# A gated mix of linear attention and a long convolution: two chunks of tokens share the transpose of q's last 64 features

## The chip, the cores and the metric

The kernel runs on one core of a Trainium2 chip. A core has five engines, each with its own in-order queue: TensorE (PE in the profile; its weight loads are listed apart as PEld), VectorE (DVE), ScalarE (ACT), GpSimd (POOL) and SyncE (SP, which here only starts DMAs). They meet through semaphores. The metric is the device time of one execution in microseconds (us). Matrix products and transposes write to PSUM, an accumulator memory of 8 banks with 2 KB in each of 128 partitions; everything else lives in SBUF.

## The reference

The input is 2048 tokens of 448 features. Branch A is linear attention with 16 heads of 28 features; branch B is a state-space convolution along the tokens; a gate per token mixes them.

```python
def _A_ref(x, wqkv, wo):
    qkv = (x @ wqkv).reshape(B, S, 3, H, Dh)      # H = 16, Dh = 28
    phi = lambda t: jnp.where(t > 0, t + 1, jnp.exp(t)) + 1e-6
    pq, pk = phi(q), phi(k)
    kv = jnp.einsum("bhsd,bhse->bhde", pk, v)
    z = jnp.einsum("bhsd->bhd", pk)
    num = jnp.einsum("bhqd,bhde->bhqe", pq, kv)
    den = jnp.einsum("bhqd,bhd->bhq", pq, z)[..., None] + 1e-6
    return (num / den).reshape(B, S, D) @ wo
...
g = sigmoid((x * gate_w).sum(-1, keepdims=True))
return g * A(x) + (1 - g) * B(x)
```

What matters here is the last part of A: phi(q), scaled by gate and denominator, times a matrix M of 448 x 448 that has been made of kv and wo.

## The kernel before, in words

The tokens are cut into 16 chunks of 128. A first part (up to about 118 us) projects q and k, and sums the products of k's features with x. A second part (118 to 127 us) makes kv and from it M. The third part, from line 814, is a loop over the 16 chunks that computes the output rows; the change lies in it and in the few lines that start it up.

Products are made at a precision above that of one pass: a number is split into a high part, rounded to the format fp32r by a copy, and a low part, the difference. A product is then high times high, low times high and high times low.

For each chunk c of the third part:

- `norm_a`, `norm_b`, `norm_d` make the reciprocal denominators: POOL multiplies q's features with the sum over k (L542), DVE sums over each head (L547), inverts two chunks at a time (L551, L553), and ACT copies the result to SBUF for POOL (L556).
- `norm_c` writes the scaled features into the tile `pn`, 128 tokens x 4 blocks of 128 columns. Blocks 0 to 2 are written by POOL (L567: 112 columns each) and DVE (L570: the last 16 columns of each). Block 3 holds the 64 features that are left, 16 of each of the last four heads, **twice** (L573, on POOL): columns 0 to 63 and again 64 to 127.
- `turn_pe` transposes the four blocks on PE into one PSUM bank of the pool `tr` (two buffers), so that features lie on partitions (L604).
- `turn_split` splits the bank: ACT copies all 512 columns to the high part `h` (L611), then DVE writes the low part `l` (L612).
- `tail` puts the gate's rows into partitions 64 to 111 of block 3 of `l` (ACT, L615).
- `attend` runs 11 matmuls of 448 columns (L629): high, low and high again of blocks 2, 0 and 1 against `mh`, `mh` and `ml`; then `h` of block 3, and `l` of block 3. In block 3 one pass over 128 partitions does two products at once: the first 64 rows of `h` meet the high part of M, the second copy of them meets M's low part, which lies in partitions 64 to 127 of `mh[:, 3]`. The first matmul needs `h`, the second needs `l`, the tenth and eleventh need block 3.
- `final_b` adds the product to y, with the gate (DVE, L634), and SP writes the rows out; `final_c` copies the product to `pq` (ACT, L640).

The order on each engine is written out by hand: the loop's body issues, for c, `norm_d` for chunks c+3 and c+4 (odd c), `final_b` of c-1, `norm_c` of c+2, `turn` of c+1, `final_c` of c-1, `tail` of c+1, `norm_a` of c+6, `attend` of c and `norm_b` of c+5. So PE transposes chunk c+1 ahead of the matmuls of chunk c, and ACT and DVE have the time of those 11 matmuls to split it. Beside this, `late` finishes the q features of the last chunk between the iterations (DVE's L799 in iteration 6, ACT's L796 in iteration 5).

"Turn c" below is the splitting of chunk c (it is issued in iteration c-1), "attend c" are the matmuls of chunk c.

Of the kernel before, what the change touches and what calls it, by code (L numbers as in the profile page):

```python
# [7 lines left out]
F32 = mybir.dt.float32  # L8
# [3 lines left out]
ALU = mybir.AluOpType  # L12
# [3 lines left out]
P = 128  # L16
S = 2048
D = 448
H = 16
DH = 28  # L20
N = 256
NC = S // P
J = 4
DJ = D // J
# [14 lines left out]
DS = 12  # L39
DT = 4 * (DH - DS)  # L40
# [100 lines left out]
def gated_mix_kernel(ctx: ExitStack, tc: tile.TileContext, xin, wq_d, wvo_d, abc_d, ldt_d, dsk_d,  # L141
                     turn_d, cst_d, first_d, gin_d, out):
    nc = tc.nc
    PE, ACT, DVE, POOL, SP = nc.tensor, nc.scalar, nc.vector, nc.gpsimd, nc.sync

    keep = ctx.enter_context(tc.tile_pool(name="keep", bufs=1))
    pq = keep.tile([P, NC, D], F32, name="pq")
# [59 lines left out]
    o = 0  # L207
    for part in PARTS:
# [8 lines left out]
        o = e  # L217
# [17 lines left out]
    def low(eng, o, r, h):  # L235
        eng.tensor_tensor(out=o, in0=r, in1=h.bitcast(F32), op=ALU.subtract)  # L236
# [301 lines left out]
    pn, th, tl, pd, dn, dp = {}, {}, {}, {}, {}, []  # L538

    def norm_a(c):  # L540
        pd[c] = tp.tile([P, D], F32, name="prod", tag="pk", bufs=3)
        POOL.tensor_tensor(out=pd[c], in0=pq[:, c], in1=zb, op=ALU.mult)  # L542
# [6 lines left out]
    def norm_d(c, n, copy=DVE.tensor_copy):  # L549
        r = dp[0][:, c:c + n]  # L550
        DVE.scalar_tensor_tensor(out=r, in0=r, scalar=1e-6, in1=e1[:, c:c + n, None].to_broadcast([P, n, H]),  # L551
                                 op0=ALU.add, op1=ALU.mult)
        DVE.reciprocal(out=r, in_=r)  # L553
        if c % 2 == 0:
            dn[c // 2] = tp.tile([P, 4, H], F32, name="den", tag="den", bufs=3)
        copy(dn[c // 2][:, c % 2:c % 2 + n], r)  # L556

    def norm_bd(c):
        norm_b(c)
        norm_d(c, 1)  # L560

    def norm_c(c):
        n = pn[c] = tp.tile([P, J, P], F32, name="pn", tag="pn")
        r = dn[c // 2][:, c % 2]
        a = pq[:, c, :3 * DJ].rearrange("p (j h d) -> p j h d", j=3, h=4)
        b = pq[:, c, 3 * DJ:].rearrange("p (h d) -> p h d", h=4)
        POOL.tensor_tensor(out=n[:, :3, :DJ].rearrange("p j (h d) -> p j h d", h=4), in0=a,  # L567
                           in1=r[:, :H - 4].rearrange("p (j h) -> p j h", j=3)[:, :, :, None].to_broadcast([P, 3, 4, DH]),
                           op=ALU.mult)
        DVE.tensor_tensor(out=n[:, :3, DJ:].rearrange("p j (h d) -> p h j d", h=4),  # L570
                          in0=b[:, :, :DS].rearrange("p h (j d) -> p h j d", j=3),
                          in1=dp[0][:, c, H - 4:, None, None].to_broadcast([P, 4, 3, DS // 3]), op=ALU.mult)
        POOL.tensor_tensor(out=n[:, 3].rearrange("p (b h d) -> p b h d", b=2, h=4),  # L573
                          in0=b[:, None, :, DS:].to_broadcast([P, 2, 4, DH - DS]),
                          in1=r[:, None, H - 4:, None].to_broadcast([P, 2, 4, DH - DS]), op=ALU.mult)

    def phi(c):
        if 0 < c < NC:
# [18 lines left out]
    def turn(c):  # L597
        turn_split(c, turn_pe(c))

    def turn_pe(c):  # L600
        o = p3.tile([P, 512], F32, name="tr", tag="tr")
        n = pn.pop(c)
        for j in range(J):
            PE.transpose(o[:, j * P:(j + 1) * P], n[:, j], ident)  # L604
        return o

    def turn_split(c, o):
        t = xt_p.tile([P, 2, J, P], F32R, name="th", tag="t")
        h, l = th[c], tl[c] = t[:, 0], t[:, 1]
        ov = o.rearrange("p (j t) -> p j t", j=J)  # L610
        ACT.copy(h, ov)  # L611
        DVE.tensor_tensor(out=l, in0=ov, in1=h.bitcast(F32), op=ALU.subtract)  # L612

    def tail(c):
        ACT.copy(tl[c][DT:RX, 3], rows[DT:RX, c * P:(c + 1) * P])  # L615
# [26 lines left out]
    c = NC - 2  # L642
# [26 lines left out]
    POOL.memset(rows[DT:RX, :D], 0.0)  # L669
    norm_bd(0)  # L670
    norm_c(0)
    norm_a(2)
    for i in range(4):
# [57 lines left out]
    def kv_split(r, kvp):  # L731
        o = kvp[:DJ, (1 - r) * 2 * DJ:(2 - r) * 2 * DJ].rearrange("p (j d) -> p j d", d=DJ)
        m = 2 - r
        DVE.tensor_tensor(out=o[:, :m], in0=kvp[:DJ, 2 * r * DJ:(2 * r + m) * DJ].rearrange("p (j d) -> p j d", d=DJ),
                          in1=mask[:, None, :].to_broadcast([DJ, m, DJ]), op=ALU.mult)
        if r:
            a, b = (w.rearrange("p (h d) -> p h d", h=4) for w in (kvp[:DJ, 3 * DJ:4 * DJ], mask))
            DVE.tensor_tensor(out=o[:, 1, :DT].rearrange("p (h d) -> p h d", h=4), in0=a[:, :, DS:], in1=b[:, :, DS:],
                              op=ALU.mult)
            a, b = (w[:, :, :DS].rearrange("p h (j d) -> p h j d", j=3) for w in (a, b))  # L740
            DVE.tensor_tensor(out=o[:, 1, DT:].rearrange("p (j h d) -> p h j d", j=3, h=4), in0=a, in1=b, op=ALU.mult)
        return o

    def kv_high(r, o):
        ACT.copy(kvh[:, 2 * r:2 * r + 2], o)
# [6 lines left out]
    k0 = kv_products(0)  # L752
    k1 = kv_split(1, k1)
    kv_high(1, k1)
    norm_c(1)
    norm_a(3)
    kv_low(1, k1)
# [11 lines left out]
    SP.dma_start(out=mh[DT:, 3].bitcast(F32), in_=shl[:DT, 1].bitcast(F32))  # L769
    m_low(2, o2)  # L770
    o0 = turn_pe(0)
    q_run(2)
    norm_a(4)
    turn_split(0, o0)
    norm_b(2)
    norm_b(3)
# [8 lines left out]
    m_low(0, o0)  # L785
    m_low(1, o1)
    norm_c(2)
    tail(0)
    q_run(11)
# [147 lines left out]
```

## Time and profile before

| | |
|---|---|
| time, median of 3 runs | 173.89 us (173.82 to 174.45) |
| the profiled execution, own time | 174.06 us |
| its span, first to last instruction | 172.2 us |
| start of attend 0, end of the last matmul | 126.87 us, 169.10 us |
| transposes (L604) | 64, 272 ns each |
| ACT's copies of 512 columns (L611) | 16, 588 ns each |
| DVE's subtractions of 512 columns (L612) | 16, 691 ns each |
| POOL's writes of block 3 (L573) | 16, 410 ns median |

The profile shows one execution. A line of its timeline gives the start and length in us, the engine, the line of the kernel, the operation, and the tiles that it writes and reads; "x10" is a run of ten, and "[0.32 <-ACT th L611]" is the time that the engine sat idle before it, and what ended that. Since matmuls are pipelined, the listed length of one is longer than the distance from one to the next. The granted TensorE clock is at full speed throughout.

### The profile page before, as it was taken

The numbers are of one execution on the slowest core, as the hardware profiler recorded it, in microseconds if no ns is written. First come the engines' busy times: TensorE is split into PE (matmuls) and PEld (weight loads), VectorE is DVE, ScalarE is ACT, GpSimd is POOL, SyncE is SP. The second block draws the span as 40 slices with busy tenths as digits, with TensorE's granted clock in tenths as the row PEclk, the third lists the DMA queues.
The fourth block names the chain that finished last, engine by engine and source line by source line (L and its number), as shares of the span: only waits on it lengthen the run. The fifth ranks groups of instructions, "written<-read, shape, count | busy, mean of one in ns | idle before, by whom it ended". The sixth has DMA issues, their size and how long they took to land. (4 is left out here: it accounts for less than half of the span.)

```text
span 172.2 us, 2796 instructions
## 1 busy us (share of the span) xinstructions
PE 167.8 (97%) x876; PEld 152.0 (88%) x876; DVE 113.9 (66%) x240; ACT 96.0 (56%) x221; POOL 120.0 (70%) x128
## 2 busy tenths in 40 slices
PE   6999999999999999999999999999999999999992
PEld 2788999999899999999999999999899999999992
DVE  0847737698975483846627346487898998987542
ACT  3688588894256262542727456356574564664541
POOL 6082667877529988696996999529968998892200
PEclk9999999999999999999999999999999999999999
DMA  5989975097003031230404200000031222122213
GB/s 173 415 297 294 268 209 166 0 368 303 4 0 114 11 123 34 95 123 1 122 15 131 106 1 1 0 0 2 7 67 54 107 89 76 62 99 107 108 59 108
DMA packets 7962, 18.60 MB, mean 108 GB/s; under 512 B 2045, under 2 KB 4810, under 8 KB 7818
## 3 DMA queue, kind: packets, MB, share of 16 engines
q1 hardware_dynamic: 7802, 18.30, 32.0%
q8 instruction: 7, 0.11, 0.3%
q10 hardware_dynamic: 144, 0.11, 0.2%
q14 instruction: 9, 0.07, 0.1%
HBM read 14.38 MB, written 3.67 MB: 105 GB/s over the span
## 5 line engine op out<-in xcount | busy, mean ns | idle before, releaser
L629 PE MATMUL a<-wk,th 128*128 128x448 f32 (+1 forms) x170 | 36.4, 360 | 0.0
L403 PE MATMUL g<-pkh,xn 128*128 128x448 f32 x112 | 35.6, 364 | 0.0
L629 PEld LDWEIGHTS a<-wk,th 128*128 128x128 f32 x170 | 29.5, 189 | 1.6
L334 PE MATMUL k<-wk,xt 128*128 128x448 f32 x132 | 29.3, 367 | 0.0
L334 PE MATMUL q<-wqh,xt 128*128 128x450 f32 x120 | 27.5, 366 | 0.0
L362 DVE SCALAR_TENSOR_TENSOR k<-k,e 128x448 f32<-128x448 f32 x12 | 7.6, 632 | 29.4 <-ACT e L361 29.4
L423 POOL TENSOR_TENSOR y<-y,t 128x448 f32<-128x448 f32 x16 | 18.7, 1168 | 11.5 <-DVE t L415 11.5
L334 PEld LDWEIGHTS k<-wk,xt 128*128 128x128 f32 x132 | 24.8, 189 | 2.2 <-DVE wk L236 0.3
L334 PEld LDWEIGHTS q<-wqh,xt 128*128 128x128 f32 x120 | 22.5, 188 | 1.7
L236 POOL TENSOR_TENSOR xn<-xr,xn 128x448 fp32r<-128x448 f32 x16 | 19.4, 1211 | 6.6 <-ACT xn L246 4.5
L403 PE MATMUL g<-pkl,xn 128*128 128x448 f32 x64 | 23.4, 366 | 0.0
L403 PEld LDWEIGHTS g<-pkh,xn 128*128 128x128 f32 x112 | 21.0, 188 | 2.2
L236 POOL TENSOR_TENSOR xt<-xr,xt 128x512 fp32r<-128x512 f32 x14 | 18.2, 1297 | 5.9 <-ACT xt L240 5.9
L360 ACT ACTIVATE e<-k 128x448 f32<-128x448 f32 x12 | 6.5, 544 | 26.9 <-PE k L334 26.9
L542 POOL TENSOR_TENSOR prod<-pq,zb 128x448 f32<-128x448 f32 x16 | 18.6, 1172 | 4.1 <-ACT zb L665 3.0
L252 POOL TENSOR_TENSOR y<-xr,rows 128x448 f32<-128x448 f32 x16 | 18.8, 1175 | 0.0
L567 POOL TENSOR_TENSOR pn<-pq,den 128x336 f32<-128x336 f32 x16 | 12.3, 771 | 5.9 <-ACT den L556 4.1
L634 DVE SCALAR_TENSOR_TENSOR ot<-y,og,a 128x448 f32<-128x448 f32 (+1 forms) x17 | 10.7, 629 | 5.1 <-PE a L629 5.1
L612 DVE TENSOR_TENSOR th<-tr,th 128x512 fp32r<-128x512 f32 x16 | 11.0, 691 | 2.7 <-ACT th L611 2.1
L403 PEld LDWEIGHTS g<-pkl,xn 128*128 128x128 f32 x64 | 11.2, 174 | 1.2 <-DVE pkl L372 0.2
L611 ACT CAST th<-tr 128x512 fp32r<-128x512 f32 x16 | 9.4, 588 | 4.6 <-PE tr L604 4.4
L334 PE MATMUL q<-wql,xt 128*128 128x450 f32 x45 | 11.6, 364 | 0.0
(150 smaller groups left out, 302.3 us busy)
## 6 DMA issues: line engine op xcount, KB each, us to landing
xr<-in SPq DMA_DIRECT2D x15, 512.0 KB, 6.2
out<-ot SPq DMA_DIRECT2D x15, 224.0 KB, 1.9
pq<-in SPq DMA_DIRECT2D x4, 448.0 KB
wvo<-in SPq DMA_DIRECT2D x1, 1792.0 KB
y<-in SPq DMA_DIRECT2D x2, 480.0 KB
y<-in SPq DMA_DIRECT2D x2, 450.0 KB
u<-t SPq DMA_DIRECT2D x30, 1.8 KB, 1.7
y<-in SPq DMA_DIRECT2D x1, 448.0 KB, 4.3
```

Of the source, the lines that this page charges most:

```text
L236: eng.tensor_tensor(out=o, in0=r, in1=h.bitcast(F32), op=ALU.subtract)
L252: POOL.tensor_tensor(out=y[:, c], in0=plain[c][:, :D], in1=dsk, op=ALU.mult)
L334: PE.matmul(o[:, :n], lhsT=a, rhs=b, start=run.n == 1, stop=not seq)
L362: DVE.scalar_tensor_tensor(out=pks[c], in0=pks[c], scalar=1.0, in1=e, op0=ALU.add, op1=ALU.max)
L403: PE.matmul(g[i][:a.shape[1], :D], lhsT=a, rhs=b, start=c == 0 and n == 0, stop=c == NC - 1 and n == len(seq) - 1)
L423: POOL.tensor_tensor(out=y[:, c], in0=y[:, c], in1=t, op=ALU.add)
L542: POOL.tensor_tensor(out=pd[c], in0=pq[:, c], in1=zb, op=ALU.mult)
L567: POOL.tensor_tensor(out=n[:, :3, :DJ].rearrange("p j (h d) -> p j h d", h=4), in0=a, in1=r[:, :H - 4].rearrange("p (j h) -> p j h", j=3)[ ...
L611: ACT.copy(h, ov)
L612: DVE.tensor_tensor(out=l, in0=ov, in1=h.bitcast(F32), op=ALU.subtract)
L629: PE.matmul(a[:, lo:hi], lhsT=u_, rhs=w_[:, lo:hi], start=n == 0, stop=n == 10)
L634: DVE.scalar_tensor_tensor(out=ot[:, lo:hi], in0=y[:, c, lo:hi], scalar=og[:, c:c + 1], in1=a[:, lo:hi], op0=ALU.mult, op1=ALU.add)
```

## The change

Block 3 is written for two chunks at once. For an even chunk c, the new `norm_pair(c)` lets POOL write 64 features of chunk c into columns 0 to 63 and the 64 features of chunk c+1 into columns 64 to 127. After the transpose, partitions 0 to 63 of the bank hold chunk c's rows, and partitions 64 to 127 hold chunk c+1's. An odd chunk transposes three blocks only.

The second copy of the 64 rows in `h` is now made by the engines that split. In an even turn ACT copies all 512 columns, then copies rows 0 to 63 of block 3 once more into partitions 64 to 127 of `h` (over the other chunk's rows). In an odd turn ACT copies the 64 rows from the bank of the chunk before, twice, into both halves of `h`'s block 3; DVE subtracts these 64 rows; then ACT and DVE do the 384 columns of the three other blocks. A list, `halves`, keeps the address of the bank's rows from the even turn to the odd one. For chunk 0 `norm_pair` is called from the start-up part, when the denominators of chunk 1 are there.

```diff
+    def norm_pair(c):
+        b = pq[:, c:c + 2, 3 * DJ:].rearrange("p b (h d) -> p b h d", h=4)
+        POOL.tensor_tensor(out=pn[c][:, 3].rearrange("p (b h d) -> p b h d", b=2, h=4), in0=b[:, :, :, DS:],
+                           in1=dn[c // 2][:, :2, H - 4:, None].to_broadcast([P, 2, 4, DH - DS]), op=ALU.mult)
+
     def norm_c(c):
...
-        POOL.tensor_tensor(out=n[:, 3].rearrange("p (b h d) -> p b h d", b=2, h=4),
-                          in0=b[:, None, :, DS:].to_broadcast([P, 2, 4, DH - DS]),
-                          in1=r[:, None, H - 4:, None].to_broadcast([P, 2, 4, DH - DS]), op=ALU.mult)
+        if c and c % 2 == 0:
+            norm_pair(c)
...
     def turn_pe(c):
         o = p3.tile([P, 512], F32, name="tr", tag="tr")
         n = pn.pop(c)
-        for j in range(J):
+        for j in range(J - c % 2):
             PE.transpose(o[:, j * P:(j + 1) * P], n[:, j], ident)
         return o
 
+    halves = []
+
     def turn_split(c, o):
+        low = lambda l, a, h: DVE.tensor_tensor(out=l, in0=a, in1=h.bitcast(F32), op=ALU.subtract)
+        ov = o.rearrange("p (j t) -> p j t", j=J)
         t = xt_p.tile([P, 2, J, P], F32R, name="th", tag="t")
         h, l = th[c], tl[c] = t[:, 0], t[:, 1]
-        ov = o.rearrange("p (j t) -> p j t", j=J)
-        ACT.copy(h, ov)
-        DVE.tensor_tensor(out=l, in0=ov, in1=h.bitcast(F32), op=ALU.subtract)
+        if c % 2:
+            b = halves.pop()
+            for p in (slice(DT, P), slice(DT)):
+                ACT.copy(h[p, 3], b)
+            low(l[:DT, 3], b, h[DT:, 3])
+            ACT.copy(h[:, :3], ov[:, :3])
+            low(l[:, :3], ov[:, :3], h[:, :3])
+        else:
+            halves.append(ov[DT:, 3])
+            ACT.copy(h, ov)
+            ACT.copy(h[DT:, 3], ov[:DT, 3])
+            low(l, ov, h)
...
     kv_high(1, k1)
+    norm_pair(0)
     norm_c(1)
```

On ACT, turns 3 and 4 stood so before, from the `tail` of chunk 2 on (`rows` is the source of `tail`, `tr` a transposed bank, `th` the tile of `h` and `l`, `a` a product, `den` the reciprocals; the numbers tell buffers apart, th_1462 being chunk 2's, th_1500 chunk 3's):

```order
L615 CAST th_1462<-rows_77 48x128
L556 COPY den_1473<-den_1276 128x32
L611 CAST th_1500<-tr_1495 128x512
L640 COPY pq_58<-a_1475 128x448
L615 CAST th_1500<-rows_77 48x128
L556 COPY den_1523<-den_1276 128x32
L611 CAST th_1537<-tr_1532 128x512
L640 COPY pq_58<-a_1508 128x448
```

The same stretch of ACT now; L627 is the old L611, L657 the old L640, L632 the old L615, and th_1501 is chunk 3's tile:

```order
L632 CAST th_1463<-rows_77 48x128
L556 COPY den_1475<-den_1276 128x32
L621 CAST th_1501<-tr_1458 64x128 x2
L623 CAST th_1501<-tr_1497 128x384
L657 COPY pq_58<-a_1477 128x448
L632 CAST th_1501<-rows_77 48x128
L556 COPY den_1527<-den_1276 128x32
L627 CAST th_1540<-tr_1535 128x512
L628 CAST th_1540<-tr_1535 64x128
L657 COPY pq_58<-a_1512 128x448
```

The odd turn 3 has three copies in place of one, the first two out of chunk 2's bank (tr_1458), and the even turn 4 has a second copy behind the first. Nothing else on ACT has changed its place.

On DVE, turns 3 and 4 before (the row of `tr` is the subtraction):

```order
L634 SCALAR_TENSOR_TENSOR ot_1488<-y_59,og_62,a_1475 128x448
L570 TENSOR_TENSOR pn_1491<-pq_58,den_1276 128x4x3x4
L612 TENSOR_TENSOR th_1500<-tr_1495,th_1500 128x512
L547 TENSOR_REDUCE den_1276<-prod_1467 128x16
L551 SCALAR_TENSOR_TENSOR den_1276<-den_1276,e1_61 128x32
L553 RECIPROCAL den_1276<-den_1276 128x32
L634 SCALAR_TENSOR_TENSOR ot_1525<-y_59,og_62,a_1508 128x448
L570 TENSOR_TENSOR pn_1528<-pq_58,den_1276 128x4x3x4
L612 TENSOR_TENSOR th_1537<-tr_1532,th_1537 128x512
```

And now:

```order
L651 SCALAR_TENSOR_TENSOR ot_1490<-y_59,og_62,a_1477 128x448
L575 TENSOR_TENSOR pn_1493<-pq_58,den_1276 128x4x3x4
L614 TENSOR_TENSOR th_1501<-tr_1458,th_1501 64x128
L614 TENSOR_TENSOR th_1501<-tr_1497,th_1501 128x384
L547 TENSOR_REDUCE den_1276<-prod_1469 128x16
L551 SCALAR_TENSOR_TENSOR den_1276<-den_1276,e1_61 128x32
L553 RECIPROCAL den_1276<-den_1276 128x32
L651 SCALAR_TENSOR_TENSOR ot_1529<-y_59,og_62,a_1512 128x448
L575 TENSOR_TENSOR pn_1532<-pq_58,den_1276 128x4x3x4
L614 TENSOR_TENSOR th_1540<-tr_1535,th_1540 128x512
```

The odd turn has two subtractions in place of one, at the same place. On POOL the write of block 3 is gone from odd chunks and follows L572 (the old L567) for even ones; for chunk 0 it has moved behind the next L542.

## The prediction, made before the changed kernel was run

> **What bounds the kernel now.** I read the page's busy times first:
>
> ```profile
> PE 167.8 (97%) x876; PEld 152.0 (88%) x876; DVE 113.9 (66%) x240; ACT 96.0 (56%) x221; POOL 120.0 (70%) x128
> ```
>
> PE is busy for 97% of the span, and DVE's 66% is a mean over stages. So I read a table by stretches, with cuts near the starts of attends 0, 6 and 10 (columns: stretch, length, then busy us of each engine):
>
> ```profile
> 126.50:142.60 16.10, 16.10 (x93) 14.91 (x92) 14.60 (x34) 9.13 (x25) 14.84 (x22) 1.00 0.24 84
> 142.60:153.20 10.60, 10.60 (x62) 9.75 (x61) 9.88 (x25) 5.54 (x15) 9.48 (x13) 1.00 0.19 72
> 153.20:172.20 19.00, 15.90 (x99) 14.80 (x97) 10.18 (x22) 8.34 (x21) 3.62 (x7) 1.00 0.26 95
> ```
>
> PE never stops in the loop, but until 153 us DVE is nearly full too: 14.60 of 16.10 us, then 9.88 of 10.60. Only the last stretch leaves it air. The waits from 118 us on say who waits for whom:
>
> ```profile
> DVE ot L634 <- PE a L629: 5.1, 7, 0.9
> ACT th L611 <- PE tr L604: 4.4, 6, 1.0
> DVE th L612 <- ACT th L611: 2.1, 7, 0.4
> PEld m L708 <- DVE kvl L748: 0.2, 1, 0.2
> ```
>
> DVE and ACT wait for PE; PE waits for nobody in the loop (its one wait, 0.2 us, is before it). So the end is set by PE's own work, as long as DVE delivers `l` in time. The prediction is a race between a shorter PE and a later DVE.
>
> **What PE gains.** From one attend to the next:
>
> ```profile
> 131.61 0.37 PE L629 MATMUL a<-rc,th 112*128 112x448 f32 x1
> 131.82 0.60 PE L604 MATMUL tr<-both,pn 128*128 128x128 f32 x4
> 132.18 2.26 PE L629 MATMUL a<-wk,th 128*128 128x448 f32 x10
> ...
> 131.62 0.57 PEld L604 LDWEIGHTS tr<-both,pn 128*128 128x128 f32 x4
> 132.15 0.30 PEld L629 LDWEIGHTS a<-wk,th 128*128 128x128 f32 x2
> ...
> 153.10 0.27 PE L589 MATMUL o<-both,og 128*1 128x128 f32 x1
> 153.22 0.60 PE L604 MATMUL tr<-both,pn 128*128 128x128 f32 x4
> ```
>
> Four transposes occupy 132.18 - 131.82 = 0.36 us, 0.09 each, although each is listed with 0.27. The loads go at (132.15 - 131.62)/4 = 0.13, and a lone extra matmul of 128 columns takes 153.22 - 153.10 = 0.12. So one transpose is worth 0.09 to 0.13 us; I take 0.09, from the matmuls themselves. Eight odd chunks lose one each: **8 x 0.09 = 0.72 us** (up to 1.06).
>
> **What the small instructions cost.** DVE and ACT rows of other sizes give the price by length:
>
> ```profile
> L612 DVE TENSOR_TENSOR th<-tr,th 128x512 fp32r<-128x512 f32 x16 | 11.0, 691 | 2.7 <-ACT th L611 2.1
> 121.65 0.39 DVE L748 TENSOR_TENSOR kvl<-k,kvh 112x224 fp32r<-112x224 f32 x1 [0.36 <-ACT kvh L745]
> 122.09 0.17 PEld L708 LDWEIGHTS m<-wo,kvl 112*112 112x112 f32 x1 [0.15 <-DVE kvl L748]
> L611 ACT CAST th<-tr 128x512 fp32r<-128x512 f32 x16 | 9.4, 588 | 4.6 <-PE tr L604 4.4
> L640 ACT COPY pq<-a 128x224 f32<-128x224 f32 x2 | 0.6, 348 | 2.0 <-DVEq L847 2.0
> 120.39 0.27 DVE L734 TENSOR_TENSOR k<-k,cst 112x112 f32<-112x112 f32 x1
> 120.70 0.23 DVE L738 TENSOR_TENSOR k<-k,cst 112x64 f32<-112x64 f32 x1
> ```
>
> DVE: (0.691 - 0.392)/288 = 1.04 ns per column, so 384 columns take 0.56 and 128 take 0.29. ACT: (0.588 - 0.348)/288 = 0.83 ns, so 384 take 0.48 and 128 take 0.27. No row shows ACT or DVE writing other partitions than it reads: I bound the 64x128 copy by nothing and by the whole 0.59, and take 0.27, the nearest by size. PE's load started 122.09 - 122.04 = 0.05 after the subtraction it waited for. An instruction that needs its predecessor on its own engine starts about 0.04 after that one's end (120.70 against 120.66); the even turn's second copy overwrites rows of the first, so it is one: **an even turn's `h` is ready 0.04 + 0.27 = 0.31 us later**, and every DVE instruction behind L612 with it.
>
> An odd turn's two small copies need nothing new and could go early, but ACT's queue is `tail`, then they, then the 384 columns. Independent ACT copies follow each other at some 0.07 us less than their length (estimate), so the two take 0.4, and the copy ends 0.4 + 0.48 - 0.59 = 0.29 later where ACT is late, and DVE's 384 columns end 0.29 - 0.13 = 0.16 later. Where DVE is itself the late one, its two subtractions cost 0.29 + 0.56 - 0.08 overlap (estimate) - 0.69 = **0.08**.
>
> The Trainium skill, Perfetto Trace Analysis, "Optimizing Scalar/DVE Operations", speaks against such splitting: each DVE instruction on PSUM carries about 125 ns of access overhead, so larger ones are to be preferred. By that price the odd turn would cost 0.125 and not 0.08, and the lag at turn 4 would be 0.05 larger; no run so far shows the split itself.
>
> **The race, turn by turn.** The rows of turns 1 and 4:
>
> ```profile
> 127.29 0.30 ACT L615 CAST th<-rows 48x128 fp32r<-48x128 f32 x1
> 127.61 0.59 ACT L611 CAST th<-tr 128x512 fp32r<-128x512 f32 x1
> 128.23 0.69 DVE L612 TENSOR_TENSOR th<-tr,th 128x512 fp32r<-128x512 f32 x1
> ...
> 135.82 0.59 ACT L611 CAST th<-tr 128x512 fp32r<-128x512 f32 x1
> 136.44 0.69 DVE L612 TENSOR_TENSOR th<-tr,th 128x512 fp32r<-128x512 f32 x1
> ...
> 137.47 0.30 PEld L629 LDWEIGHTS a<-wk,th 128*128 128x128 f32 x2
> ```
>
> In turn 1 ACT goes straight from `tail` to the copy, so it is the late one: lag 0.16. In turn 2 ACT waits for PE, which is 0.09 earlier: lag 0.31 - 0.09 = 0.22. Turn 3 adds 0.08: 0.30. In turn 4 L612 started 0.03 after ACT's copy: + 0.31, so **lag 0.61**. Attend 4 loads `l` as its second weight, at 137.47 + 0.30 - 0.19 = 137.58; `l` was ready at 137.13 + 0.05: slack 0.40. PE therefore ends turn 4 at 0.61 - 0.40 = 0.21 *after* its old time, having spent the 0.27 of turns 1, 3 and 5. Part of this is paid one step earlier: the transposes of chunk 4 overwrite the bank of chunk 2, which DVE's small subtraction of turn 3 still reads; the 11 matmuls of attend 3 queue behind them.
>
> From turn 5 to 7 DVE catches up (it waits for PE there), and PE gains 2 x 0.09 by turn 9. Now turns 8 and 10:
>
> ```profile
> 144.54 1.23 POOL L542 TENSOR_TENSOR prod<-pq,zb 128x448 f32<-128x448 f32 x1
> 144.97 1.05 DVE L799 TENSOR_SCALAR t<-e 128x448 f32<-128x448 f32 x1
> 147.33 0.69 DVE L612 TENSOR_TENSOR th<-tr,th 128x512 fp32r<-128x512 f32 x1
> 148.11 0.30 PEld L629 LDWEIGHTS a<-wk,th 128*128 128x128 f32 x2
> 152.35 0.69 DVE L612 TENSOR_TENSOR th<-tr,th 128x512 fp32r<-128x512 f32 x1
> 153.54 0.30 PEld L629 LDWEIGHTS a<-wk,th 128*128 128x128 f32 x2
> ...
> L350 DVE TENSOR_SCALAR t<-e x15: 384/593/1382, 20.5 to 115.2; 128x448 f32<-128x448 f32 x15
> ```
>
> L799 took 1.05 us, while the same operation in L350 takes from 0.38: it ended 0.25 after POOL's L542, which it met. POOL now skips 0.41 (L573) in each odd chunk, four of them by then, so I expect L542 to be over: L799 then gives back 0.66. Following DVE on from turn 4 in the same way leaves it 0.58 late at L799, 0.08 early behind it, + 0.31 and small change for the even turn: lag 0.29, slack 148.22 - 148.02 - 0.05 = 0.15, so PE stands at +0.14. Turns 9 and 10 have DVE working without a pause, lag 0.66 against a slack of 153.65 - 153.04 - 0.05 = 0.56: PE at +0.10. From there DVE has room (10.18 of 19.00 us), and odd chunks 13 and 15 still give 0.18. **Sum: +0.10 - 0.18 = -0.08 us**: 0.72 gained, 0.64 lost to waits at attends 4, 8 and 10.
>
> What costs nothing: POOL's eight writes less (3.3 us), since PE waits for none of them; `norm_pair(0)` behind one more L542, ready near 121.5 and needed at 122.80 (were it later than that, PE would wait one for one). No DMA is moved.
>
> The profiled execution took 174.06, 1.83 more than its span of 172.23, and 0.17 more than the median of 173.89. 174.06 - 0.08 = 174.0; against the median **173.8 us**. What a measurement can tell from no change is some 0.5%, 0.87 us.
>
> **Rivals.** *The whole gain comes through.* If ACT's small copies slip into its idle time and DVE's lag stays under 0.13 at turn 4, no attend waits: 173.89 - 0.72 = 173.2, down to 172.8 at 0.13 per transpose. For it: ACT is busy only 9.13 of 16.10 us; against it: in L612's rows DVE starts right behind ACT in even turns. 23%, a third of it beyond 0.5%.
>
> *The lock stays.* If DVE reaches L799 while POOL is in L542 again, its 0.66 isn't given back: the lag at turn 8 is 0.95, PE stands at +0.80 there, about +0.7 behind attend 10, and +0.5 at the end: 174.4. The Trainium skill, SBUF — State Buffer, "Who interferes with whom", has the rule: whoever issues first holds the shared port pair for its whole instruction, the other fully blocks. By that rule it is one or the other and nothing between; the rows of L542 and L799 agree. 14%.
>
> *Copies to other partitions are dear.* Were L621 and L628 as long as 128x512, 0.59, every even turn would lag 0.32 more, and odd ones up to 0.6 where ACT is late; it decides from turn 4 on, where the slack is 0.40. Lag at turn 4 some 1.3, PE +0.9; at turn 10 as much again; at the end about +1.1: 175.0. Nothing in the trace speaks for it but that no row excludes it. 8%, slower by over 0.5%.
>
> That the removed transposes are free anyway (PE waiting for the next load) is spoken against by L589, which moved the period by 0.12; I leave it inside the first case.
>
> **How the numbers follow.** 55% for the forecast, with 0.25 us either way for the lag: 173.5 to 174.2. With the rivals: faster by over 0.5% 8% (a third of the first), slower 10% (the third, and 2 of the lock's 14), within 82%. The range, from the full gain with something over 0.09 per transpose to behind the lock rival: 173.0 to 174.6.
>
> **What would show it.** Three transposes in odd chunks, periods of 2.57 and 2.66 us where nothing waits; weight loads of attends 4, 8 and 10 waiting for DVE; L628 at 0.27, 0.04 behind L627; L817 (the old L799) at about 0.4. It is wrong if PE shows no wait in the loop, if L817 still takes 1 us, or if PE waits in attends 12 to 15.

## The result, and the profile after

| | time, median | ratio to before, 95% interval |
|---|---|---|
| before, same chip | 173.98 us (13 runs) | |
| after | 174.62 us (13 runs) | 1.0034 (1.0023 to 1.0045) |

The change costs 0.59 us (0.40 to 0.78: the ratio and its interval, times 173.98): it is slower, by less than 0.5%. The forecast of 173.8 is missed by 0.8 us, and the range by 0.02.

The profiled execution of after took 175.03 us, 0.97 more than that of before. Only a part of this is the change's. The first transposes and the last matmul of after, from the timeline of PE:

```profile
123.47 0.60 PE L608 MATMUL tr<-both,pn 128*128 128x128 f32 x4
...
169.85 0.27 PE L646 MATMUL a<-rc,th 112*128 112x224 f32 x1
```

Before they stood at 123.00 and 168.83. So 0.47 is there when the loop starts; it comes up within the first 8 us, where ACT's L265 and L439 wait longer for the input. Two runs below with the same start-up (runs 1 and 4) have their first transposes at 122.99 and 122.71, so I put the 0.47 down to the execution and not to the change. The loop itself, from the first row to the second, took 45.83 us before and 46.38 after: **+0.55**. All loop figures below are differences of this length to before, one execution each. Beside them stands the ratio of the times, of which 0.0010 is 0.17 us. The two agree to 0.15 us (after: +0.55 beside +0.59), in run 5 to 0.3 and in run 8, with a single time on each side, to 0.2.

The busy times of after, then the three stretches of the prediction (columns: stretch, length, busy us of PE, PEld, DVE, ACT, POOL; the loop of after starts 0.47 later in them):

```profile
PE 168.2 (97%) x868; PEld 150.7 (87%) x868; DVE 114.7 (66%) x248; ACT 102.2 (59%) x245; POOL 117.3 (68%) x120
```
```profile
126.50:142.60 16.10, 15.93 (x89) 14.15 (x88) 14.46 (x36) 10.52 (x31) 13.74 (x17) 1.00 0.22 72
142.60:153.20 10.60, 10.45 (x58) 9.20 (x57) 9.39 (x26) 6.93 (x21) 8.60 (x11) 1.00 0.23 89
153.20:172.20 19.00, 16.92 (x101) 15.35 (x99) 11.93 (x28) 11.88 (x33) 3.75 (x6) 1.00 0.26 98
```

The page's totals don't show the loss: PE is still busy for 97%. In the stretches PE now has holes up to 153 us, of 0.17 and 0.15, where there were none (more is hidden in the modelled ends of matmuls). The waits from 122 us on name them (us in total, times, longest):

```profile
PEld a L646 <- DVE th L614: 0.9, 3, 0.4
PEld tr L608 <- issue: 0.8, 2, 0.5
...
PE tr L608 <- DVE th L614: 0.2, 1, 0.2
PE a L646 <- DVE th L614: 0.2, 1, 0.2
...
DVE th L614 <- ACT th L628: 2.6, 6, 0.6
```

Before, PE waited for nobody in the loop. Now it waits for DVE's low parts, and DVE for ACT's second copy. Where PE waits, from its timeline and that of its weight loads:

```profile
132.41 2.25 PE L646 MATMUL a<-wk,th 128*128 128x448 f32 x10
134.51 0.37 PE L646 MATMUL a<-rc,th 112*128 112x448 f32 x1
135.03 0.63 PE L608 MATMUL tr<-both,pn 128*128 128x128 f32 x4 [0.16 <-DVE th L614]
```
```profile
138.42 1.70 PEld L646 LDWEIGHTS a<-wk,th 128*128 128x128 f32 x9 [0.29 <-DVE th L614]
...
149.24 1.70 PEld L646 LDWEIGHTS a<-wk,th 128*128 128x128 f32 x9 [0.44 <-DVE th L614]
...
154.87 1.31 PEld L646 LDWEIGHTS a<-wk,th 128*128 128x128 f32 x7 [0.18 <-DVE th L614]
```

These are the transposes of chunk 4 and the second weight loads of attends 4, 8 and 10. Where nothing waits, the end of one attend lies 2.545 us behind that of the last if three blocks are transposed between, and 2.655 if four are: a transpose is worth 0.11. Whatever a distance has beyond that is lost:

| lost at | us |
|---|---|
| transposes of chunk 4 (bank of chunk 2 still read) | 0.35 |
| attend 4 | 0.27 |
| attend 8, and transposes of chunk 10 behind it | 0.58 |
| attend 10 | 0.17 |
| attend 12 | 0.12 |
| **sum** | **1.49** |

The gain is 8 x 0.11 = 0.88. What is left, 1.49 - 0.88 = +0.61, is the loop's +0.55 to within the reading of these distances.

### The profile page after: what moved, and what is told of

Read it like the earlier page. It is cut to its first block, busy times and chain, and to the rows that moved or that the text cites. A ratio compares the mean times of both kernels' runs of the same rounds, so it can differ in the third digit from the quotient of the medians.

```text
span 173.3 us, 2793 instructions
## 1 busy us (share of the span) xinstructions
PE 168.2 (97%) x868; PEld 150.7 (87%) x868; DVE 114.7 (66%) x248; ACT 102.2 (59%) x245; POOL 117.3 (68%) x120
## 5 line engine op out<-in xcount | busy, mean ns | idle before, releaser
L646 PE MATMUL a<-wk,th 128*128 128x448 f32 (+1 forms) x170 | 37.2, 363 | 0.2 <-DVE th L614 0.2
L542 POOL TENSOR_TENSOR prod<-pq,zb 128x448 f32<-128x448 f32 x16 | 18.5, 1160 | 4.5 <-ACT zb L682 3.0
L572 POOL TENSOR_TENSOR pn<-pq,den 128x336 f32<-128x336 f32 x16 | 12.2, 761 | 8.5 <-ACT den L556 7.6
L614 DVE TENSOR_TENSOR th<-tr,th 128x512 fp32r<-128x512 f32 (+2 forms) x24 | 12.3, 514 | 4.3 <-ACT th L628 2.6
L366 ACT ACTIVATE pkh<-k 128x448 fp32r<-128x448 f32 x12 | 6.6, 546 | 8.5 <-DVE k L362 8.5
```

What stands on the lines that cost most here:

```text
L366: ACT.add(pkh[c], pks[c], 1e-6)
L614: low = lambda l, a, h: DVE.tensor_tensor(out=l, in0=a, in1=h.bitcast(F32), op=ALU.subtract)
L646: PE.matmul(a[:, lo:hi], lhsT=u_, rhs=w_[:, lo:hi], start=n == 0, stop=n == 10)
```

## The experiments

**The theory after the result.** PE's gain is real. DVE, which had no air up to 153 us, loses more than it has: in even turns by the wait for the second copy, in odd turns by a small subtraction that costs far more than predicted. The rivals: the gain was never there; one of the two costs alone does it; what makes the small subtraction dear is its number, or that it writes other partitions than it reads, or where it starts.

Eight kernels ran. "Loop" is as above.

| run | edit | time | ratio to before | loop, us |
|---|---|---|---|---|
| 1 | second copy of even turns behind DVE's subtraction | 173.68 | 0.9984 (0.9973 to 0.9996) | -0.41 |
| 2 | before, three transposes in odd chunks | 173.20 | 0.9962 (0.9943 to 0.9982) | -0.69 |
| 3 | after, with the removed transposes back | 174.74 | 1.0046 (1.0030 to 1.0063) | +0.81 |
| 4 | small copies and subtraction in their own partitions | 173.82 | 0.9983 (0.9970 to 0.9996) | -0.45 |
| 5 | 1 and 4 together | 173.54 | 0.9971 (0.9958 to 0.9983) | -0.80 |
| 6 | no small subtraction; all copies in the even `tail` | 173.99 | 0.9999 (0.9988 to 1.0011) | -0.09 |
| 7 | as 6, two copies moved behind the odd turn's big one | 173.34 | 0.9958 (0.9939 to 0.9976) | -0.69 |
| 8 | 4 and one more small subtraction, one execution | 175.60 | (one time each; before 174.49) | +1.31 |

**Run 1: the second copy later.**

```diff
-    halves = []
+    halves, again = [], {}
...
             ACT.copy(h, ov)
-            ACT.copy(h[DT:, 3], ov[:DT, 3])
             low(l, ov, h)
+            again[c] = ov[:DT, 3]
 
     def tail(c):
+        if c in again:
+            ACT.copy(th[c][DT:, 3], again.pop(c))
```

> The changed kernel with one move: in an even turn DVE's subtraction follows ACT's 512-column copy directly, and the second copy of the 64 rows is made later, just ahead of tail's rows. Theory A (DVE comes late; 0.31 us of it in each even turn is the wait for the second copy, 0.31 in each odd turn is the small subtraction, which overlaps neither neighbour): L614 of even turns starts 0.03 after L627 as before the change; the waits of attends 4, 8 and 10 mostly go, some wait at the transposes of chunks 4 or 10 may stay; 0.6 to 1.0 us faster than the changed kernel, so 173.6 to 174.0. Rival B (the small subtraction and the shared bank alone hold PE): at most 0.3 us faster, 174.3 to 174.6. Rival C (the loop isn't what differs): no change, 174.6.

First after, turn 4, from the timelines of ACT and DVE; then DVE in turn 4 of run 1:

```profile
136.76 0.59 ACT L627 CAST th<-tr 128x512 fp32r<-128x512 f32 x1
137.39 0.26 ACT L628 CAST th<-tr 64x128 fp32r<-64x128 f32 x1
```
```profile
137.68 0.69 DVE L614 TENSOR_TENSOR th<-tr,th 128x512 fp32r<-128x512 f32 x1 [0.41 <-ACT th L628]
```
```profile
136.66 0.19 DVE L575 TENSOR_TENSOR pn<-pq,den 128x48 f32<-128x48 f32 x1
136.97 0.69 DVE L614 TENSOR_TENSOR th<-tr,th 128x512 fp32r<-128x512 f32 x1
```

In after DVE starts 0.03 behind L628, which itself starts 0.04 behind L627's end: 0.04 + 0.26 where 0.04 + 0.27 was predicted. In run 1 DVE follows the 512 columns, without that wait. The loop is 0.96 shorter than after's, and no attend waits for DVE any more; what is left are hold-ups at the transposes of chunks 4 and 10. So the even turn's wait is a cause. It isn't the only one: run 1 still falls 0.47 short of the full 0.88. The late copy (L633) and `tail` (L634) stand so on ACT in turn 4 of run 1; the last section comes back to them:

```profile
137.70 0.26 ACT L633 CAST th<-tr 64x128 fp32r<-64x128 f32 x1 [0.32 <-DVE th L614]
137.86 0.29 ACT L634 CAST th<-rows 48x128 fp32r<-48x128 f32 x1
```

**Run 2: the gain alone.**

```diff
-        for j in range(J):
+        for j in range(J - c % 2):
...
+        if c % 2:
+            v = o[:, :3 * P]
+            ov = bass.AP(tensor=v.tensor, offset=v.offset, ap=[v.ap[0], [85, J], [1, P]])
```

> The kernel before with three transposes in odd chunks, and nothing else of the change; odd chunks' fourth block is read as an overlapping view of the other three, so that the rows of odd chunks are not the reference's while every copy and subtraction keeps its size. It prices PE's gain alone. Theory A: PE is the bound and no new wait comes: 8 x 0.11 = 0.88 us faster than before, 173.1. Rival (a removed transpose is worth less, 0 to 0.05, as PE then waits for its next load or for l): 173.6 to 174.0.

The loop is 0.69 shorter and the time, by its ratio, 0.66. One wait of attends is left in it, from the waits of run 2:

```profile
PEld a L632 <- DVE th L615: 0.2, 1, 0.2
```

That is attend 8: 0.88 - 0.2 = 0.68. The gain of 0.11 per transpose is there, and even the old DVE work only just keeps up with it.

**Run 3: the transposes back.**

```diff
-        for j in range(J - c % 2):
-            PE.transpose(o[:, j * P:(j + 1) * P], n[:, j], ident)
+        for j in range(J):
+            PE.transpose(o[:, j * P:(j + 1) * P], n[:, min(j, J - 1 - c % 2)], ident)
```

> The changed kernel, with a fourth transpose in odd chunks again (block 2 once more, into columns that nobody reads). Theory A: while DVE sets the pace (turns 1 to 10) the added 0.11 us are hidden in PE's waits, and only those of chunks 13 and 15, and perhaps one or two more, show: 0.2 to 0.45 us slower than the changed kernel, 174.8 to 175.1. Rival C (PE sets the pace throughout, the loss is elsewhere): the full 0.88 slower, 175.5.

Eight transposes of 0.11 add 0.88 of PE's work, and the loop grows by 0.26 over after's; the median of 174.74 lies just under the 174.8 expected at least. Attends 4 and 8 still wait for DVE. So in after most of a shorter PE goes into waiting: DVE sets the pace between turns 4 and 10, whatever PE does.

**Run 4: each half stays where it is.**

```diff
             for p in (slice(DT, P), slice(DT)):
-                ACT.copy(h[p, 3], b)
-            low(l[:DT, 3], b, h[DT:, 3])
+                ACT.copy(h[p, 3], b[p])
+            low(l[:DT, 3], b[:DT], h[:DT, 3])
...
-            halves.append(ov[DT:, 3])
+            halves.append(ov[:, 3])
```

> The changed kernel, where the odd turn's small subtraction reads and writes partitions 0 to 63 alone, and its two small copies stay in the partitions they read; the block-3 rows of odd chunks are then those of the chunk before, so their output isn't the reference's. It asks what makes the small subtraction 0.31 us dear. Theory A1 (an instruction with a start at partition 64 doesn't overlap its neighbours): the small L614 starts 0.12 after L575 and the next 0.2 after it, each odd turn is 0.2 shorter on DVE, and the run is 0.3 to 0.6 us faster than the changed kernel. Rival A2 (any instruction on fewer than 128 partitions, or any so short, stands alone): starts 0.23 and 0.32 apart as in the changed kernel, same time, 174.6.

The odd turn on DVE, first turn 5 of after, then turn 5 of run 4 (L614 x2 is the small subtraction and the one of 384 columns):

```profile
139.40 0.20 DVE L575 TENSOR_TENSOR pn<-pq,den 128x48 f32<-128x48 f32 x1
139.63 0.88 DVE L614 TENSOR_TENSOR th<-tr,th 64x128 fp32r<-64x128 f32 x2
140.43 0.62 DVE L547 TENSOR_REDUCE den<-prod 128x16 f32<-128x448 f32 x1
```
```profile
138.42 0.20 DVE L575 TENSOR_TENSOR pn<-pq,den 128x48 f32<-128x48 f32 x1
138.54 0.74 DVE L614 TENSOR_TENSOR th<-tr,th 64x128 fp32r<-64x128 f32 x2
139.20 0.61 DVE L547 TENSOR_REDUCE den<-prod 128x16 f32<-128x448 f32 x1
```

From L575's start to that of the sum behind (L547) it is 140.43 - 139.40 = 1.03 in after and 139.20 - 138.42 = 0.78 in run 4. Before, in turn 3, the rows say 0.72:

```profile
133.73 0.20 DVE L570 TENSOR_TENSOR pn<-pq,den 128x48 f32<-128x48 f32 x1
133.85 0.69 DVE L612 TENSOR_TENSOR th<-tr,th 128x512 fp32r<-128x512 f32 x1
134.45 0.62 DVE L547 TENSOR_REDUCE den<-prod 128x16 f32<-128x448 f32 x1
```

So the split costs **+0.31** in after and +0.06 in run 4, near the predicted 0.08. The instructions are no longer than thought. What differs is when they start: in run 4 the small one starts 0.08 before L575's end (138.62), in after 0.03 behind it (139.63 against 139.60). On ACT the same pair of copies stands in front of the 384 columns; after first, then run 4:

```profile
128.17 0.54 ACT L621 CAST th<-tr 64x128 fp32r<-64x128 f32 x2
128.73 0.48 ACT L623 CAST th<-tr 128x384 fp32r<-128x384 f32 x1
```
```profile
127.41 0.53 ACT L621 CAST th<-tr 64x128 fp32r<-64x128 f32 x2
127.85 0.47 ACT L623 CAST th<-tr 128x384 fp32r<-128x384 f32 x1
```

0.56 against 0.44. The loop is 1.00 shorter than after's, more than the 0.3 to 0.6 expected, although the even turns still wait for L628. Each of the two causes alone, taken away, turns the loss into a gain. Run 4 takes away DVE's 0.25 and ACT's 0.12 together. In turns 3, 5, 9 and 15 of after DVE is the late one and its own time counts; in turns 1, 7, 11 and 13 it waits for ACT's 384 columns (L623). What each of the two is worth alone wasn't measured.

**Run 5: both.** Edits 1 and 4 in one kernel.

> The changed kernel with both edits: the even turn's second copy late, just ahead of tail's rows, and the odd turn's small instructions in the partitions that they read (block-3 rows of odd chunks are those of the chunk before, so their output isn't the reference's). Theory A (the two delays of DVE are all that ate PE's gain): nearly the whole 0.88 us of three transposes against the kernel before, 173.1 to 173.3, with at most one short wait of PE in turns 1 to 10. Rival D (a third delay, such as the shared bank or ACT's longer queue, keeps a part): no better than the better of the two edits alone, 173.6 to 173.8.

The loop is 0.80 shorter than before's; the weight loads of attends wait for nobody, and only the transposes of chunk 4 are held up, by 0.1 of PE's time (0.88 - 0.80). By the loop the two causes together account for nearly the whole of the lost gain. The ratio shows less of it, 0.50 us (0.30 to 0.73), and the median of 173.54 lies between what theory A and rival D had. The granted clock bears on that: in six of run 5's twelve executions it was 0.996 to 0.998, with a median of 173.62, and the other six have 173.18, which is 0.77 below the kernel before (under 0.999 in one of its 23). Whether the clock is the reason isn't shown: in after, the three executions at 0.997 and 0.998 weren't the slow ones (174.39 to 174.53). The row of the first stretch in run 5 shows that the gain isn't there because DVE has less to do:

```profile
126.50:142.60 16.10, 16.10 (x92) 14.70 (x91) 14.91 (x38) 10.59 (x35) 14.38 (x19) 1.00 0.24 83
```

DVE has 14.91 busy us in place of 14.46 in a stretch of the same 16.10: what was taken away are gaps.

**Runs 6 and 7: a complete version without the small subtraction.** DVE makes the low part of the whole bank in the even turn, for both chunks; ACT copies the other chunk's half across. (The lines of after that go are left out here.)

```diff
+        if c % 2 == 0:
+            for k in (c, c + 1):
+                t = xt_p.tile([P, 2, J, P], F32R, name="th", tag="t")
+                th[k], tl[k] = t[:, 0], t[:, 1]
+            again[c] = ov[:, 3]
+        m = J - c % 2
+        h, l = th[c], tl[c]
+        ACT.copy(h[:, :m], ov[:, :m])
+        low(l[:, :m], ov[:, :m], h[:, :m])
...
     def tail(c):
+        b = again.pop(c, None)
+        if b is not None:
+            ACT.copy(tl[c + 1][:DT, 3], tl[c][DT:, 3].bitcast(F32))
+            ACT.copy(th[c][DT:, 3], b[:DT])
         ACT.copy(tl[c][DT:RX, 3], rows[DT:RX, c * P:(c + 1) * P])
+        if b is not None:
+            for p in (slice(DT, P), slice(DT)):
+                ACT.copy(th[c + 1][p, 3], b[DT:])
```

> A version meant to keep the gain and the whole computation: in an even turn DVE subtracts the whole bank before the second copy, so that the low part of the next chunk's 64 rows comes out of the same 512 columns; ACT then, with tail, copies that low part and the high part to the next chunk's tile, and the odd turn keeps one copy and one subtraction of 384 columns. DVE has no small subtraction and no wait for the second copy; ACT has one small copy more per pair, three of them moved from the odd turn into the even tail. Theory A: PE waits for nobody in the loop, 8 x 0.11 us gained against before: 173.1 to 173.2. Rival E (ACT's tail, about 1.4 us long in even turns now, makes the odd turn's 384-column copy late, and PE waits in attends 3, 5 or 9): 173.4 to 174.0.

Run 6 is level with before, as rival E had it. Four small copies and `tail`'s rows now stand in ACT's queue ahead of the odd turn's 384 columns, and DVE waits for those. Its turn 1 on ACT, DVE's answer, and the weight load of attend 1:

```profile
128.41 0.54 ACT L634 CAST th<-tr 64x128 fp32r<-64x128 f32 x2
128.97 0.48 ACT L623 CAST th<-tr 128x384 fp32r<-128x384 f32 x1
```
```profile
129.48 0.56 DVE L614 TENSOR_TENSOR th<-tr,th 128x384 fp32r<-128x384 f32 x1 [0.96 <-ACT th L623]
```
```profile
130.09 1.70 PEld L648 LDWEIGHTS a<-wk,th 128*128 128x128 f32 x9 [0.19 <-DVE th L614]
```

Attend 8 waits for DVE in the same way, 0.28, and the transposes of chunk 4 wait 0.44 for POOL's write of block 3 (L564). Nothing of the work in L634 is needed by DVE, so run 7 puts it behind L623, in the odd turn (against run 6):

```diff
         ACT.copy(h[:, :m], ov[:, :m])
+        if c % 2:
+            for p in (slice(DT, P), slice(DT)):
+                ACT.copy(h[p, 3], again[c - 1][DT:])
         low(l[:, :m], ov[:, :m], h[:, :m])
...
-        if b is not None:
-            for p in (slice(DT, P), slice(DT)):
-                ACT.copy(th[c + 1][p, 3], b[DT:])
```

> The version of e6 with ACT's small copies spread: the low part of the next chunk's 64 rows and the second copy of this chunk's stay in the even tail (0.3 us more there than in e1), the two copies of the high part go behind the odd turn's 384-column copy, where attend needs them last. Nothing is left out of the computation. Theory A (DVE's lateness alone costs PE time, and in e6 it came from ACT's 384-column copy standing behind five small ones): the loop is some 0.8 us shorter than before, PE waits at most once; 173.1 to 173.4, the fastest of the complete versions. Rival E2 (ACT, with one small copy more per pair and each of them standing alone, is itself the late one): attends 1, 3 or 9 still wait for the odd turn's subtraction, 173.6 to 174.0, no better than e1.

```profile
129.61 0.42 PEld L608 LDWEIGHTS tr<-both,pn 128*128 128x128 f32 x4 [0.34 <-issue]
```

One hold-up of note is left in run 7, this one. The profile names no releaser for it; the transposes of chunk 2 overwrite chunk 0's bank, which ACT's moved copies were reading until 129.54. At 173.34 us against 174.12, ratio 0.9958 (0.9939 to 0.9976), it is the fastest version that computes all of the output: 0.73 us below the kernel before. Its interval doesn't part it from runs 2 and 5, and meets that of run 1 at its edge.

**Run 8: what makes the small subtraction dear.** Run 4 changed two things at once, where the instruction starts and that it stays in its partitions. Run 8 keeps run 4 and adds a subtraction that reads and writes partitions 64 to 127.

```diff
             low(l[:DT, 3], b[:DT], h[:DT, 3])
+            low(l[DT:, 3], b[DT:], h[DT:, 3])
```

> The kernel of e4 with one more small subtraction on DVE in each odd turn: after the one in partitions 0 to 63 stands one that reads and writes partitions 64 to 127 and crosses nothing (its result is overwritten by tail; block-3 rows of odd chunks are those of the chunk before, so their output isn't the reference's). It tells two readings of A1 apart by the distances on DVE. If a start at partition 64 is what forbids overlap: the added one starts 0.03 after the end of the first, and the 384-column one 0.03 after the end of the added one, about 0.30 and 0.32 apart. If crossing from one half to the other is what forbids it: both follow their predecessor by about 0.2, as the first does in e4. The time, some 0.2 us above e4, decides nothing.

Three stretches of DVE's timeline in turn 3, the small subtraction from partition 0, the one from 64, and the sum behind the 384 columns:

```profile
134.11 0.20 DVE L575 TENSOR_TENSOR pn<-pq,den 128x48 f32<-128x48 f32 x1
134.23 0.28 DVE L614 TENSOR_TENSOR th<-tr,th 64x128 fp32r<-64x128 f32 x1
```
```profile
134.52 0.29 DVE L614 TENSOR_TENSOR th<-tr,th 64x128 fp32r<-64x128 f32 x1
```
```profile
134.52 0.88 DVE L614 TENSOR_TENSOR th<-tr,th 64x128 fp32r<-64x128 f32 x2
...
135.32 0.62 DVE L547 TENSOR_REDUCE den<-prod 128x16 f32<-128x448 f32 x1
```

From partition 0: 0.12 behind L575's start, as any other. From 64: 0.29 later, behind its predecessor's end (134.51), and the pair from 134.52 again takes 0.88, as in after. It crosses no partitions, so the cost doesn't need a crossing. L575 to L547 is 1.21, and 1.21 - 0.78 = 0.43 for one instruction of 0.29. The loop is 1.76 longer than run 4's, where some 0.2 was expected: on an engine without air, eight times 0.43 doesn't stay hidden.

## Why the prediction failed

**PE's gain.** Mechanism right, size small: 0.11 per transpose and not 0.09, 0.88 and not 0.72 in all. Run 2 shows it.

**The even turn, "0.04 + 0.27 = 0.31 us later".** Right: 0.04 + 0.26, and run 1 shows what it is worth, 0.96 us of the loop. With it fell the rival of dear copies: across partitions ACT took 0.26, and in place as well.

**The odd turn, "its two subtractions cost ... 0.08".** This is the term that failed. It measured +0.31. The sum took an overlap of 0.08 for granted on the small subtraction, as DVE's other neighbours have it. The small subtraction reads from partition 64, and in after it has none on either side; on partitions 0 to 63, in run 4, it has. The 0.125 that the Trainium skill gives per DVE instruction on PSUM (Perfetto Trace Analysis, "Optimizing Scalar/DVE Operations") lies between the measured numbers and fits neither: 0.31 in after, 0.06 in run 4. The same mistake on ACT made "the two take 0.4" into 0.56.

The trace of before had a row that could have warned. Partitions 64 to 111 of `rc` were written there by L699; these are DVE's neighbours around it:

```profile
121.96 0.39 DVE L734 TENSOR_TENSOR tr<-tr,cst 112x224 f32<-112x224 f32 x1
122.38 0.69 DVE L699 SCALAR_TENSOR_TENSOR rc<-zs,cst,z 48x448 fp32r<-48x448 f32 x1
123.10 0.39 DVE L748 TENSOR_TENSOR kvl<-tr,kvh 112x224 fp32r<-112x224 f32 x1
123.41 0.61 DVE L716 TENSOR_TENSOR shl<-m,shl 112x448 fp32r<-112x448 f32 x1
```

L716 starts 0.08 before L748's end. L699 starts 0.03 behind L734's end, and L748 0.03 behind its own. I read the overlap from the first kind and priced an instruction of the second. On ACT the prediction's own rows of turn 1 have it: `tail`, on partitions 64 to 111, ends at 127.59, and L611 starts at 127.61.

**The race.** It was the right picture, with that term too small. How much later than before DVE ends each low part, less the 0.47 of the start:

| | turn 1 | turn 2 | turn 3 | turn 4 | start of L799, now L817 | turn 8 |
|---|---|---|---|---|---|---|
| predicted | 0.16 | 0.22 | 0.30 | 0.61 | 0.58 | 0.29 |
| measured | 0.41 | 0.16 | 0.47 | 0.77 | 1.07 | 0.69 |

In turn 1 ACT is the late one, and 0.16 of what was missed there is its pair of small copies; by turn 2, where ACT waits for PE, that is gone. Turn 3 is the first odd turn in which DVE is the late one, and there the two part for good: 0.31 added in place of 0.08. Turn 5 adds 0.13, and in turn 6 DVE waits 0.41 for L628 and is 1.13 late. So DVE doesn't catch up as "from turn 5 to 7 DVE catches up" had it; it loses more. The waits came where they were forecast, at the bank of chunk 2 and at attends 4, 8 and 10, and the small one at attend 12, which was named as a sign against the prediction. They cost 1.49, and not the 0.64 that the sum had.

**The lock.** The rival fell, but the forecast's term held by luck as much as by its reason. POOL and DVE in turn 7 of after:

```profile
144.88 1.17 POOL L542 TENSOR_TENSOR prod<-pq,zb 128x448 f32<-128x448 f32 x1
```
```profile
146.51 0.38 DVE L817 TENSOR_SCALAR t<-e 128x448 f32<-128x448 f32 x1
```

POOL was done at 146.05, and L817 took 0.38 instead of 1.05, as expected; that gave DVE back 0.67, of which turn 8's wait for the second copy takes a part again: the drop from 1.07 to 0.69 in the table. But less the 0.47 of the start POOL's end is only 0.20 earlier than before, while DVE came 1.07 later. With the lag of 0.58 that was forecast, L817 would have started within 0.02 of POOL's end. In runs 2 and 7, where DVE isn't that late, the two still meet. In run 2 the same operation took 1.38, from 144.42 to 145.80, and POOL's L542 ended at 145.55. In run 7, where it is L818:

```profile
144.06 1.16 POOL L542 TENSOR_TENSOR prod<-pq,zb 128x448 f32<-128x448 f32 x1
144.92 0.54 DVE L818 TENSOR_SCALAR t<-e 128x448 f32<-128x448 f32 x1
```

In before and in both of these runs DVE's instruction ends some 0.25 behind POOL's, whenever it started; it is 1.05, 1.38 and 0.54 long. That agrees with the rule that the Trainium skill has in SBUF — State Buffer, "Who interferes with whom": the one that issues first keeps the shared pair for its whole instruction, and the other blocks. But it isn't "one or the other and nothing between", as the prediction read it: how long the wait is goes by what is left of POOL's instruction.

**The range.** Its upper end was put 0.2 behind the lock rival's 174.4. A case in which the odd turn is dear on DVE wasn't in it, since the text bounded the copies to other partitions from both sides but not the overlap, which was an estimate with one value.

## What to carry to other kernels

When work leaves a full engine, look at what the engine next to it has to do in the same period: here 0.88 us of PE's time were freed by giving DVE and ACT small instructions, and DVE had hardly a gap to put them in. Price a small instruction by the distance from its predecessor's start to its successor's, read from an instruction on the same partitions, and not by its length. An edit that copies something twice should issue the copy that others wait for first; moving two copies behind the big one (run 7 against run 6) was worth 0.6 us without any change in the work.

## What the hardware showed that was not expected

- Whether an instruction on DVE or ACT overlaps its neighbours depends in these runs on the partitions it works on. On partitions from 0 on, and without a wait between them, the second starts before the first one's end, by some 0.08 us on DVE and 0.10 on ACT. A DVE instruction that reads from partition 64 on, between such neighbours, starts 0.01 to 0.03 us behind its predecessor's end, and its successor 0.03 behind its own. That is so for the subtractions of 64x128 (after, run 8: both sides) and for L699 of 48x448; the subtraction of 64x128 from partition 0 (run 4) overlaps on both sides.
- On ACT the partitions that are read are not the whole condition. In turn 4 of after L628, which reads from partition 0 and writes from 64, ends at 137.65, and the next copy, L657, starts 0.02 behind that. In turn 4 of run 1 `tail`, which reads and writes from 64, starts 0.10 before the end of such a copy (L634 at 137.86, L633's end at 137.96). So the partitions that are written count too. No run has such a pair on DVE; what the full condition is, and why, stays open.
- The first inputs can arrive some 0.5 us earlier or later from one execution to the next (ACT's L439 started at 7.07 in before, 7.54 in after and 6.77 in run 4), so that a single profiled execution can't tell a change of 0.6 us by its own time; the length of the loop could.
